# Attention with top-k and two gated MLPs on one core: keys stored once and queries split twice, a fold factor kept, weight stores on SP, another scheduler

## The chip, the cores and the metric

The kernel runs on one core of one Trainium2 chip. The metric is the device time in microseconds of one execution. A core has TensorE (PE, with its weight loads PEld), VectorE (DVE), ScalarE (ACT), GpSimd (POOL) and SyncE (SP), and 16 DMA engines that serve the transfers issued by SP and ScalarE.

## The reference

```python
# attention: q, k, v of (4, 8, 576, 64)
scores = scale * np.matmul(q, k.transpose(0, 1, 3, 2))
kth = np.partition(scores, -32, axis=-1)[..., -32:-31]
scores = np.where(scores >= kth, scores, -1000000000.0)
attn = np.exp(scores - max); attn = attn / (sum + 1e-09)
x = np.matmul(attn, v)            # heads side by side: (2304, 512)
# first MLP: w_in (512, 2048), w_out (2048, 512)
h = x @ w_in; x = (h * sigmoid(h)) @ w_out
# second MLP: w1, w2 (512, 1024), w3 (1024, 1024), w4 (1024, 512)
out = (((x @ w1) * (x @ w2)) @ w3) @ w4
```

For each query only the 32 largest scores of a row of 576 count. All is float32.

## The kernel before

The 2304 tokens are cut into six blocks of three row tiles of 128, that is 384 tokens each; a batch has 576 tokens, so blocks cross batches. For each block the eight heads' attention gives 24 (head, row tile) items, taken in 12 pairs; then comes the block's MLP work. The pairs' attention runs ahead: while block j goes through the MLPs, block j+1 goes through attention.

**Precision.** Most matmuls run in the format fp32r, with each operand split in a rounded part and a remainder; three products (rounded x rounded, rounded x remainder, remainder x rounded) give the result. For the scores the 64-wide heads leave half of the 128 partitions free: queries lie in tile `qs` with the rounded part in the lower 64 partitions and the remainder in the upper 64; keys lie in `kk` as two planes, rounded and remainder, each stored twice over the partitions. Two matmuls of 288 columns give half a row of scores. A batch's keys, where a later block needs them again, are written to DRAM (`kscr`) and read back into `kk` (`load_qk`, `cached_k`, `split_qk`, `go`).

**Top-k.** `plan_topk`: VectorE takes the 8 largest of a row four times (`mx`), erasing them in between (`mr`). ScalarE masks and exponentiates into `e`, VectorE adds and takes the reciprocal `rc` (`recip`), one for each pair. `norm` then makes ready what the transposes need.

**Attention output.** `plan_av`: `tr` transposes the probabilities on TensorE, `ev` evicts them, `mm` multiplies by v. Blocks 0 and 1 are "native": plain float32, with two heads' v in one tile `vn`. In block 0 (`DIAG`) a transpose is a matmul by the diagonal tile `dg` = identity x `rc`, which scales as it transposes; in block 1 `norm` scales `e` itself and a transpose by `ident` follows. The result becomes `xh` and `xl`, the MLP's input.

**Weights.** In block 0 the weights come raw from DRAM and are split by `conv_step(k)`: load (SP), two ScalarE passes, a GpSimd clamp, VectorE's joining of bits, ScalarE's rounding and GpSimd's subtraction into a piece `wt`. Each of the 48 finished pieces (512 KB) is stored to DRAM (`scr`) from ScalarE's queue and read back by all later blocks (`stream`). Loads of raw weights share a ring of four buffers (`RB`); pieces have two rings of three (`WT`, tags w0 and w1).

**Fold.** `fold_steps` computes w3 @ w4 once, in two halves of eight jobs, so the second MLP ends in one matmul less; its remainder is `w4l`. The factor w4 is converted in the first half, stored to DRAM (`scr4`, ScalarE's queue) and read back from SP into `w4r` for the second.

**Order.** All of this is recorded first as a list of operations with modelled costs (`Recorder`). `schedule` then looks for an order: `forward` is a list scheduler that gives start times from a rank, `backward` gives a new rank from these, and of 24 rounds the rank with the least sum of three jittered cases is kept. Instructions are emitted in the order of their start times, so each engine's queue, and SP's with all its loads, runs in that order. Line 457 of the profile is the line that emits them all; so the rows are told apart by tiles.

Of the kernel before, what the change touches and what calls it, by code (L numbers as in the profile page):

```python
# [29 lines left out]
KB = 3  # L30
# [8 lines left out]
ROUNDS = 24  # L39
CASES = 3  # L40
ENGINES = ("sync", "scalar", "vector", "gpsimd", "tensor")
WAKE = (17, 24, 24, 70, 44)
POOL, PE = 3, 4
NATIVE = lambda j: j < 2
# [165 lines left out]
class Recorder:  # L210
# [52 lines left out]
    def graph(self):  # L263
        ops = self.ops
        self.needs = [sorted(o.needs) for o in ops]
        self.heirs, self.after = [[] for _ in ops], [[] for _ in ops]
        index, self.key, self.turn, ahead = {}, [], [], {}
        self.users, self.takes = [], [[] for _ in ops]
        for n, o in enumerate(ops):
            for k in self.needs[n]:  # L270
                self.heirs[k].append(n)
            for k in sorted(o.weak):
                self.after[k].append(n)
            for t in o.takes:
# [8 lines left out]
        self.tiles = [[index[t] for t in o.tiles] for o in ops]  # L283
        self.engine = [ENGINES.index(o.engine) for o in ops]
        self.wake = [WAKE[e] for e in self.engine]

    def queues(self, rank, takes, turn, left, gap):
        given, spare = dict.fromkeys(self.caps, 0), {k: [0.] * c for k, c in self.caps.items()}
        got, parked, avail = [None] * len(self.key), {}, [0.] * len(self.ops)
        later, ready, free = [[] for _ in ENGINES], [[] for _ in ENGINES], [0.] * len(ENGINES)  # L290
        key, engine = self.key, self.engine

        def offer(n):
# [9 lines left out]
            for t in takes[n]:  # L303
                if got[t] is None:
                    got[t] = heapq.heappop(spare[key[t]])
                    given[key[t]] += 1
                if got[t] > 0.:
                    avail[n] = max(avail[n], got[t] + gap(n))
# [8 lines left out]
        def back(t, when):  # L317
            heapq.heappush(spare[key[t]], when)
            wake(key[t])
# [16 lines left out]

    def forward(self, rank, hold, done):
        ops, engine = self.ops, self.engine
        left = [len(o.needs) + len(o.weak) for o in ops]
        offer, back, pick, avail, free = self.queues(rank, self.takes, self.turn, left, lambda n: 0.)  # L340
        users, lastuse = [len(u) for u in self.users], [0.] * len(self.key)
        start, total = [0.] * len(ops), 0.
        wire = busy = held = 0.
        for _ in ops:
            t, e, ready = pick()
            n = heapq.heappop(ready)[1]
            late = 0.
            if ops[n].shares and busy > t + AVOID:
                aside = [n]
                while ready and ops[ready[0][1]].shares:  # L350
# [4 lines left out]
            if ops[n].shares:  # L355
                late = max(0., busy - t)
                held = t + late + hold[n]
            elif e == POOL:
                late = max(0., held - t)
                busy = t + late + hold[n]  # L360
            start[n] = t
            free[e] = t + late + hold[n]
            end = t + late + done[n]
            if ops[n].dma:
                wire = max(wire, t + 1400) + done[n]
                end = wire + 1050
            total = max(total, end)
# [58 lines left out]
    def jitter(self, dice, amount):  # L426
        hold, done = [], []
        for o in self.ops:
            f = 1. + amount * (2. * dice.random() - 1.)
            hold.append(o.hold if o.dma else o.hold * f + (0. if o.engine == "tensor" else 8.))  # L430
            done.append(o.done * (1. + 3. * amount * dice.random()) if o.dma else o.done * f + 8.)
        return hold, done

    def schedule(self):
        self.graph()
        dice = random.Random(7)
        cases = [self.jitter(dice, 0.04) for _ in range(CASES)]

        def cost(rank):
            return sum(self.forward(rank, *c)[1] for c in cases)  # L440

        rank = list(range(len(self.ops)))
        least = cost(rank)
        for _ in range(ROUNDS):
            times = self.jitter(dice, dice.choice((0., 0.02, 0.05)))
            r = rank
            for _ in range(2):
                r = self.backward(self.forward(r, *times)[0], *times)
                c = cost(r)
                if c < least:  # L450
                    least, rank = c, r
        start, _ = self.forward(rank, [o.hold for o in self.ops], [o.done for o in self.ops])
        return [self.ops[n] for n in sorted(range(len(start)), key=lambda n: (start[n], n))]

# [6 lines left out]
def attention_moe_moe2_kernel(  # L461
# [77 lines left out]

    def convert_bits(t, u, n=-1):  # L540
        w = raw_p.tile([128, 512], FP32, tag="w", bufs=WB, name="w")
        if MERGE(n):
# [19 lines left out]
    scr = [dram.tile([128, 2, 512], FP32, name=f"scr{i}") for i in range(NH)]  # L562
    scr4 = [dram.tile([128, DM], FP32, name=f"scr4_{i}") for i in range(NI)]
    piece = {}
# [10 lines left out]
    def conv_step(k):  # L575
# [23 lines left out]
    def fold_steps():  # L599
# [8 lines left out]
        st = {}  # L608
        cur = {}
        accs = []  # L610
# [3 lines left out]
        def mm(n):  # L614
            kind, half, j, _ = jobs[n]
            w = st.pop(n)
            if kind == "b":
                cur[j] = w
                nc.scalar.dma_start(out=scr4[j], in_=w)
                return  # L620
            if half == 0:
                b_ = cur.pop(j)
            else:
                b_ = cur.pop(("r", j))
            if j == 0:
# [17 lines left out]
        def step(k):  # L643
# [7 lines left out]
            if 0 <= a < len(jobs):  # L651
                st[a] = convert_bits(*st[a])
# [103 lines left out]
    def cached_v(j, h):  # L756
        t0, T = blocks[j]
        hd = heads[j, h]
        if NATIVE(j):
# [32 lines left out]
    def plan_scores(n, base):  # L792
# [9 lines left out]
        def go(tick, j, h, i, half, si, r0, r1):  # L802
# [498 lines left out]
```

## Time and profile before

| | us |
|---|---|
| median of 3 runs | 1127.8 (1127.1 to 1129.38) |
| profiled execution, its own time | 1130.65 |
| its span, first to last instruction | 1128.8 |
| TensorE busy | 1080.0 (96%) |
| VectorE busy | 898.1 (80%) |
| ScalarE busy | 851.6 (75%) |
| GpSimd busy | 745.1 (66%) |

In the rows, `out<-in` names the tiles that an instruction writes and reads, `xN` is a count, ACTq and SPq are the issues of transfers from ScalarE's and SP's queue. Issues are not in the engines' busy times. A matmul's end is modelled and neighbours overlap, so distances between starts say more than lengths.

### The profile page before, as it was taken

How to read it: one execution, taken by the hardware profiler on the slowest of the kernel's cores; microseconds unless marked ns; L12 is line 12 of the kernel's file. 1: busy time of each engine (PE TensorE's matmuls, PEld its weight loads, DVE VectorE, ACT ScalarE, POOL GpSimd, SP SyncE). 2: the span in 40 equal slices, each digit the busy share in tenths (PEclk: the TensorE clock that was granted, in tenths of full speed). 3: DMA queues.
4: the chain of work that ended last, by engine and by line, in shares of the span. 5: the costliest groups of instructions: out<-in, count | busy, mean ns of one | idle time of the engine just before them, and what ended most of it. 6: DMA issues, size and time to landing. Idle time of an engine off the chain costs nothing.

```text
span 1128.8 us, 19547 instructions
## 1 busy us (share of the span) xinstructions
PE 1080.0 (96%) x6096; PEld 983.9 (87%) x6096; DVE 898.1 (80%) x2062; ACT 851.6 (75%) x1911; POOL 745.1 (66%) x766
## 2 busy tenths in 40 slices
PE   4899997898899999999999999999999999999998
PEld 3555567787889999999999999999999999999997
DVE  7999999897979999998999988888899999401100
ACT  5899889888988878878878887888787788642221
POOL 4678557788886677867777766867766666542221
PEclk9899989999999999999999999999999999999999
DMA  8876479989898786767778667897857776358740
GB/s 278 255 251 217 136 251 313 304 299 353 278 325 318 240 239 211 268 195 233 249 265 284 232 198 249 295 311 275 280 169 256 244 235 197 131 159 253 252 167 28
DMA packets 127879, 273.53 MB, mean 242 GB/s; under 512 B 40480, under 2 KB 65056, under 8 KB 127776
## 3 DMA queue, kind: packets, MB, share of 16 engines
q1 hardware_dynamic: 119712, 245.02, 67.2%
q10 hardware_dynamic: 8064, 27.27, 6.1%
q8 instruction: 49, 0.80, 0.3%
q14 instruction: 54, 0.44, 0.1%
HBM read 216.14 MB, written 56.10 MB: 241 GB/s over the span
## 4 chain that ended last, share of the span: by engine, by line
PE 63%; DVE 17%; ACT 9%; POOL 5%; issue 4%; DMA 1%; ACTq 0%; SPq 0%; POOLq 0%; DVEq 0%
PE bank L457 63%; DVE top L457 7%; DVE wk L457 6%; ACT e L457 3%; DVE gf L457 2%; POOL wt L457 1%; ACT st L457 1%; POOL gl L457 1%; POOL t L457 1%; POOL e L457 1%; ACT t L457 1%; ACT wt L457 1%; ACT pf L457 0%; DMA raw<-in_w_dram 0%; ACT ph L457 0%
## 5 line engine op out<-in xcount | busy, mean ns | idle before, releaser
L457 DVE MAX8 top<-wk 128x8 f32<-128x576 f32 x432 | 319.5, 753 | 4.6
L457 POOL TENSOR_TENSOR gl<-gf,gh 128x384 fp32r<-128x384 f32 x144 | 147.6, 1025 | 165.7 <-ACT gh L457 159.9
L457 PE MATMUL bank<-xh,wt 128*128 128x384 f32 x768 | 221.4, 341 | 2.6 <-ACT st L457 2.6
L457 PE MATMUL bank<-gh,wt 128*128 128x384 f32 x768 | 221.9, 341 | 0.2 <-ACT gh L457 0.2
L457 PE MATMUL bank<-x2h,wt 128*128 128x384 f32 x768 | 217.3, 341 | 1.4 <-ACT wt L457 1.1
L457 DVE MATCH_REPLACE8 wk<-top,wk 128x576 f32<-128x576 f32 x288 | 213.4, 742 | 0.0
L457 PE MATMUL bank<-kk,qs 128*128 128x288 f32 x640 | 148.1, 321 | 21.8 <-ACT kk L457 12.0
L457 POOL TENSOR_TENSOR pl<-pf,ph 128x384 fp32r<-128x384 f32 x128 | 129.8, 1021 | 37.8 <-ACT ph L457 35.4
L457 ACT ACTIVATE st<-bank 128x288 f32<-128x288 f32 (+1 forms) x320 | 127.4, 410 | 34.3 <-PE bank L457 31.6
L457 PEld LDWEIGHTS bank<-kk,qs 128*128 128x128 f32 x640 | 114.6, 196 | 39.0 <-issue 11.0
L457 PEld LDWEIGHTS bank<-xh,wt 128*128 128x128 f32 x768 | 141.9, 189 | 3.5 <-ACT st L457 2.8
L457 PEld LDWEIGHTS bank<-x2h,wt 128*128 128x128 f32 x768 | 140.5, 188 | 4.1 <-ACT wt L457 1.3
L457 PEld LDWEIGHTS bank<-gh,wt 128*128 128x128 f32 x768 | 140.5, 189 | 1.6 <-ACT gh L457 0.6
L457 PE MATMUL bank<-gl,wt 128*128 128x384 f32 x384 | 131.5, 342 | 3.0 <-POOL gl L457 2.9
L457 DVE MAX8 top<-st 128x8 f32<-128x576 f32 x144 | 107.9, 751 | 31.5 <-ACT st L457 30.6
L457 PE MATMUL bank<-xl,wt 128*128 128x384 f32 x384 | 129.6, 338 | 1.1 <-POOL xl L457 1.1
L457 PE MATMUL bank<-x2l,wt 128*128 128x384 f32 x384 | 129.0, 337 | 0.3 <-POOL x2l L457 0.3
L457 ACT ACTIVATE e<-st,top 128x576 f32<-128x576 f32 x144 | 108.6, 777 | 21.4 <-DVE top L457 19.1
L457 POOL TENSOR_SCALAR e<-e,rc 128x640 f32<-128x640 f32 (+1 forms) x120 | 95.1, 801 | 40.7 <-DVE rc L457 17.5
L457 ACT CAST gh<-gf 128x384 fp32r<-128x384 f32 x144 | 74.2, 515 | 61.5 <-DVE gf L457 60.7
L457 ACT ACTIVATE e<-e,nb 128x576 f32<-128x576 f32 x144 | 111.7, 778 | 0.4 <-issue 0.3
L457 DVE SCALAR_TENSOR_TENSOR gf<-th,bank 128x384 f32<-128x384 f32 x96 | 52.4, 546 | 73.9 <-ACT th L457 72.1
(82 smaller groups left out, 2334.7 us busy)
## 6 DMA issues: line engine op xcount, KB each, us to landing
wt<-scr SPq DMA_DIRECT2D x240, 512.0 KB, 4.3
scr<-wt ACTq DMA_DIRECT2D x48, 512.0 KB, 5.4
k<-kk SPq DMA_DIRECT2D x32, 576.0 KB, 4.6
kk<-k SPq DMA_DIRECT2D x32, 576.0 KB, 5.3
raw<-in_w_dram SPq DMA_DIRECT2D x24, 512.0 KB, 5.6
kr<-in_kT_dram SPq DMA_DIRECT2D x32, 288.0 KB, 4.9
raw<-in_w3T_dram SPq DMA_DIRECT2D x16, 512.0 KB, 5.3
raw<-in_w_in_dram SPq DMA_DIRECT2D x16, 512.0 KB, 6.0
```

Source lines behind the costliest of these rows:

```text
L457: o.call(*[real_ap(x) for x in o.args], **{k: real_ap(x) for k, x in o.kw.items()})
```

## The change

- The scheduler: `forward` now takes the order in which buffers are handed out (`turns`) from the new rank, holds back a transfer while eight are under way, and doubles TensorE's times in stretches that follow little work. A new `replay` times a fixed order in four jittered cases, and the best order itself is kept (before, the best rank).
- Keys are one plane: rounded part in the lower partitions, remainder in the upper. Queries are two planes, rounded and remainder, each over all 128 partitions. A stored or reloaded `kk` has half the bytes.
- The fold's converted w4 stays in four `wt` tiles (`kept`); its stores and loads go.
- In `cached_v` one load fetches the last 64 rows of v for both heads.
- `DIAG` is false: block 0 scales `e` and transposes by identity, as block 1 does.
- The 48 stores of weight pieces are issued from SP.

```diff
-CASES = 3
+CASES = 4
+SEED = 8
+LANES = 8
...
-DIAG = lambda j: j == 0
+DIAG = lambda j: False
...
+STORE = lambda a: True
...
+    def turns(self, start):
+        turn, seen = [0] * len(self.key), {}
+        for t in sorted(range(len(turn)), key=lambda t: (start[self.taker[t]], self.taker[t], t)):
+            turn[t] = seen[self.key[t]] = seen.get(self.key[t], -1) + 1
+        return turn
...
+                if slow:
+                    h, d = 2. * h, d + h
+                filled += h
...
+            elif dma[n]:
+                late = max(0., lanes[lane] - t)
...
+                lanes[lane] = end = wire + 1050
+                lane = (lane + 1) % LANES
...
+    def replay(self, order, prior, hold, done, phase):
...
+        for n in order:
+            e = engine[n]
+            t, wake = free[e], wakes[n]
+            for k in self.needs[n]:
+                x = off[k] if e == PE and engine[k] == PE else end[k] + wake
+                if x > t:
+                    t = x
+            for x in self.takes[n]:
+                if prior[x] >= 0 and release[prior[x]] > t:
+                    t = release[prior[x]]
...
+        return total
 
     def schedule(self):
         self.graph()
-        dice = random.Random(7)
-        cases = [self.jitter(dice, 0.04) for _ in range(CASES)]
...
+        dice = random.Random(SEED)
+        cases = [self.jitter(dice, 0.03) for _ in range(CASES)]
+        plan, least, best = (list(range(len(self.ops))), self.turn), None, None
+
+        def trial(p, times):
+            nonlocal plan, least, best
+            start, _ = self.forward(p, *times)
+            order, prior = sorted(range(len(start)), key=lambda n: (start[n], n)), self.prior
+            c = sum(self.replay(order, prior, *x) for x in cases)
+            if least is None or c < least:
+                plan, least, best = p, c, order
+            return start
...
+            p = plan
             for _ in range(2):
...
+                rank = self.backward(trial(p, times), *times[:2])
+                p = rank, self.turns(rank)
+            trial(p, plain)
+        return [self.ops[n] for n in best]
...
-            nc.scalar.dma_start(out=scr[a], in_=piece[0, a].bitcast(FP32))
+            (nc.sync if STORE(a) else nc.scalar).dma_start(out=scr[a], in_=piece[0, a].bitcast(FP32))
...
-                cur[j] = w
-                nc.scalar.dma_start(out=scr4[j], in_=w)
                 return
...
+            b_ = kept[j // 2][:, j % 2]
...
-                if half == 1:
-                    b_ = wt_p.tile([128, 2, 512], FP32, tag=f"w{j % 2}", name="w4r")[:, 0]
-                    nc.sync.dma_start(out=b_, in_=scr4[j])
-                    cur["r", j] = b_
+                if kind == "b" and j % 2 == 0:
+                    kept.append(wt_p.tile([128, 2, 512], FP32, tag=f"w{j // 2 % 2}", name="w4f"))
+                st[a] = convert_bits(*st[a], w=kept[j // 2][:, j % 2] if kind == "b" else None)
...
-            kk = kv_p.tile([128, 2, S], FP32R, tag="k", bufs=KB, name="kk")
+            kk = kv_p.tile([128, S], FP32R, tag="k", bufs=KB, name="kk")
...
-        qs = kv_p.tile([128, T], FP32R, tag="qs", name="qs")
-        nc.scalar.copy(out=qs, in_=qr)
+        qs = kv_p.tile([128, 2, T], FP32R, tag="qs", name="qs")
+        nc.scalar.copy(out=qs[:, 0], in_=qr)
...
-        sub(out=qs[D:D2], in0=qr[D:D2], in1=qs[D:D2])
+        sub(out=qs[:, 1], in0=qr, in1=qs[:, 0])
...
-                nc.scalar.copy(out=kk[:, 0], in_=kr)
-                sub(out=kk[:, 1], in0=kr, in1=kk[:, 0])
+                nc.scalar.copy(out=kk, in_=kr)
+                sub(out=kk[D:D2], in0=kr[D:D2], in1=kk[D:D2])
                 if s + n < S:
-                    kscr[b, h] = dram.tile([128, 2, S], FP32, name=f"k{b}_{h}")
+                    kscr[b, h] = dram.tile([128, S], FP32, name=f"k{b}_{h}")
...
-                    nc.sync.dma_start(out=vt[0:REM, NFULL, x], in_=v[b, h + x, NFULL * 128:S])
+                nc.sync.dma_start(out=vt[0:REM, NFULL], in_=v[b, h:h + 2, NFULL * 128:S].rearrange("x p d -> p x d"))
...
-            q_ = hd["q"][:, i * 128:(i + 1) * 128]
-            nc.tensor.matmul(ps[:, 0:HS], lhsT=q_, rhs=kk[:, 0, cs], start=True, stop=False)
-            nc.tensor.matmul(ps[:, 0:HS], lhsT=q_, rhs=kk[:, 1, cs], start=False, stop=True)
+            for x in range(2):
+                nc.tensor.matmul(ps[:, 0:HS], lhsT=hd["q"][:, x, i * 128:(i + 1) * 128], rhs=kk[:, cs],
+                                 start=(x == 0), stop=(x == 1))
```

## Rows read from the trace of the kernel before

**Rows 1.** The page, part 1: busy us by engine, share of the span, instructions.

```profile
PE 1080.0 (96%) x6096; PEld 983.9 (87%) x6096; DVE 898.1 (80%) x2062; ACT 851.6 (75%) x1911; POOL 745.1 (66%) x766
```

**Rows 2.** Table by stage: stretch, length, busy us by engine, clock, DMA share, GB/s.

```profile
0.00:160.00 160.00, 137.38 (x538) 84.05 (x539) 148.90 (x348) 131.64 (x282) 99.34 (x109) 0.96 0.73 234
160.00:340.00 180.00, 158.94 (x892) 143.47 (x891) 156.50 (x334) 156.28 (x334) 147.85 (x143) 0.98 0.89 304
340.00:640.00 300.00, 299.95 (x1806) 290.91 (x1805) 280.95 (x660) 250.83 (x582) 223.78 (x231) 1.00 0.76 248
640.00:960.00 320.00, 318.58 (x1954) 307.95 (x1953) 283.82 (x664) 256.69 (x599) 219.82 (x229) 1.00 0.75 247
960.00:1128.00 168.00, 165.15 (x914) 157.47 (x912) 27.89 (x61) 56.18 (x118) 54.33 (x55) 1.00 0.52 166
```

**Rows 3.** Chain of waits from 0 to 160 us, shares by line.

```profile
by line: PE bank L457 70.5%; issue 4.2%; DMA raw<-in_w_dram 3.4%; POOL w L457 3.0%; DVE top L457 2.9%; ACT e L457 2.9%; DVE wk L457 2.7%; ACT st L457 2.7%; ACT t L457 1.5%; ACT pn L457 1.0%; ACT bank L457 0.8%; ACT wt L457 0.7%; SPq L457 0.
```

**Rows 4.** Chain of waits from 160 to 340 us, shares by line.

```profile
by line: PE bank L457 23.9%; issue 9.4%; POOL wt L457 8.6%; DVE top L457 5.4%; DVE wk L457 5.3%; POOL t L457 4.6%; ACT e L457 4.3%; POOL gl L457 3.9%; POOL e L457 3.6%; DMA k<-kk 2.8%; ACT wt L457 2.7%; ACT t L457 2.7%; ACT bank L457 2.3%; 
```

**Rows 5.** VectorE's timeline: start, length, the 12th and the 24th reciprocal.

```profile
156.28 0.14 DVE L457 RECIPROCAL rc<-rc 128x2 f32<-128x2 f32 x1
...
350.79 0.15 DVE L457 RECIPROCAL rc<-rc 128x2 f32<-128x2 f32 x1
```

**Rows 6.** Instructions of the tile xh: ns min/median/max, first and last start.

```profile
L457 PE MATMUL bank<-xh,wt x768: 331/334/656, 167.7 to 1069.1; 128*128 128x384 f32 x192
```

**Rows 7.** Groups by line, TensorE: count, busy us, mean ns, idle before.

```profile
L457 PE MATMUL bank<-ident,e 128*128 128x128 f32 x600 | 100.4, 274 | 7.9 <-ACT st L457 5.4 <-POOL e L457 1.5 <-ACT pn L457 0.7
...
L457 PE MATMUL bank<-dg,e 128*128 128x128 f32 (+1 forms) x240 | 35.8, 286 | 1.1 <-ACT st L457 1.0
```

**Rows 8.** TensorE's timeline at 68 us: start, length, what, count.

```profile
68.55 1.50 PE L457 MATMUL bank<-dg,e 128*128 128x128 f32 x12
69.80 0.51 PE L457 MATMUL bank<-kk,qs 128*128 128x288 f32 x2
```

**Rows 9.** Groups by line and shape, GpSimd and ScalarE, whole span.

```profile
L457 POOL TENSOR_TENSOR gl<-gf,gh 128x384 fp32r<-128x384 f32 x144 | 147.6, 1025 | 165.7 <-ACT gh L457 159.9 <-PE bank L457 4.3
...
L457 ACT ACTIVATE e<-st,top 128x576 f32<-128x576 f32 x144 | 108.6, 777 | 21.4 <-DVE top L457 19.1 <-POOL wt L457 1.3
...
L457 POOL TENSOR_TENSOR qs<-qr,qs 64x384 fp32r<-64x384 f32 x47 | 48.1, 1024 | 12.8 <-ACT qs L457 6.8 <-issue 3.1
...
L457 POOL TENSOR_SCALAR e<-e,rc 128x576 f32<-128x576 f32 x24 | 18.5, 778 | 4.6 <-ACT bank L457 2.1 <-DVE rc L457 1.4
...
L457 POOL TENSOR_SCALAR dg<-ident,rc 128x128 f32<-128x128 f32 x16 | 6.2, 394 | 7.7 <-DVE rc L457 7.0
...
L457 ACT ACTIVATE dg<-ident,rc 128x128 f32<-128x128 f32 x8 | 3.1, 407 | 0.0
```

**Rows 10.** Instructions of the tiles scr and w4l: ns min/median/max, first and last.

```profile
L457 ACTq DMA_DIRECT2D scr<-wt x48: 326/326/474, 144.4 to 360.1; - x48
...
L457 POOL TENSOR_TENSOR w4l<-wf,w4h x8: 1269/1277/1290, 93.4 to 141.6; 128x512 fp32r<-128x512 f32 x8
```

**Rows 11.** DMA issues between 160 and 340 us: count, KB each, us to landing.

```profile
scr<-wt ACTq DMA_DIRECT2D x40, 512.0 KB, 5.4
...
kk<-k SPq DMA_DIRECT2D x8, 576.0 KB, 6.4
k<-kk SPq DMA_DIRECT2D x6, 576.0 KB, 6.2
```

**Rows 12.** Waits between 160 and 340 us: total us, times, longest.

```profile
POOL t L457 <- ACT t L457: 8.3, 6, 4.5
DVE gf L457 <- ACT th L457: 8.2, 4, 3.7
...
DVE w L457 <- POOL t L457: 7.1, 8, 2.0
```

**Rows 13.** SP's timeline of issues at 215 us: start, length, what, count.

```profile
215.43 7.00 SPq L457 DMA_DIRECT2D vn<-in_v_dram  x6
```

More of the change, by code (lines that the diff above doesn't have):

```diff
@@ L43 @@
 POOL, PE = 3, 4
+WINDOW, FULL = 3413., 0.55
 NATIVE = lambda j: j < 2
-DIAG = lambda j: j == 0
+DIAG = lambda j: False
 EARLY = lambda j, h: j == 0 and h == 0
@@ L283, in graph @@
         self.tiles = [[index[t] for t in o.tiles] for o in ops]
+        self.taker = [n for n, o in enumerate(ops) for _ in o.takes]
+        self.shares = [o.shares for o in ops]
+        self.dma = [o.dma for o in ops]
         self.engine = [ENGINES.index(o.engine) for o in ops]
@@ L287, in queues @@
     def queues(self, rank, takes, turn, left, gap):
-        given, spare = dict.fromkeys(self.caps, 0), {k: [0.] * c for k, c in self.caps.items()}
+        given, spare = dict.fromkeys(self.caps, 0), {k: [(0., -1)] * c for k, c in self.caps.items()}
         got, parked, avail = [None] * len(self.key), {}, [0.] * len(self.ops)
+        prior = self.prior = [-1] * len(self.key)
         later, ready, free = [[] for _ in ENGINES], [[] for _ in ENGINES], [0.] * len(ENGINES)
@@ L304, in offer @@
                 if got[t] is None:
-                    got[t] = heapq.heappop(spare[key[t]])
+                    got[t], prior[t] = heapq.heappop(spare[key[t]])
                     given[key[t]] += 1
-                if got[t] > 0.:
+                if prior[t] >= 0:
                     avail[n] = max(avail[n], got[t] + gap(n))
@@ L317, in back @@
         def back(t, when):
-            heapq.heappush(spare[key[t]], when)
+            heapq.heappush(spare[key[t]], (when, t))
             wake(key[t])
@@ L335, in queues, with forward @@
         return offer, back, pick, avail, free
[L337 to L340, printed above, removed]
+    def turns(self, start):
[3 more added lines that the diff above has]
+        return turn
+    def forward(self, plan, hold, done, phase):
+        rank, turn = plan
+        engine, dma, shares = self.engine, self.dma, self.shares
+        left = [len(o.needs) + len(o.weak) for o in self.ops]
+        offer, back, pick, avail, free = self.queues(rank, self.takes, turn, left, lambda n: 0.)
         users, lastuse = [len(u) for u in self.users], [0.] * len(self.key)
-        start, total = [0.] * len(ops), 0.
+        start, total = [0.] * len(left), 0.
         wire = busy = held = 0.
-        for _ in ops:
+        window, filled, slow = 0, 0., True
+        lanes, lane = [0.] * LANES, 0
+        for _ in left:
             t, e, ready = pick()
@@ L347, in forward @@
             late = 0.
-            if ops[n].shares and busy > t + AVOID:
+            if shares[n] and busy > t + AVOID:
                 aside = [n]
-                while ready and ops[ready[0][1]].shares:
+                while ready and shares[ready[0][1]]:
                     aside.append(heapq.heappop(ready)[1])
@@ L354, in forward @@
                     heapq.heappush(ready, (rank[x], x))
-            if ops[n].shares:
-                late = max(0., busy - t)
-                held = t + late + hold[n]
+            h, d = hold[n], done[n]
+            if e == PE:
+                w = int((t + phase) // WINDOW)
+                while window < w:
+                    slow = filled < WINDOW * FULL
+                    filled = max(0., filled - WINDOW)
+                    window += 1
+                if slow:
+                    h, d = 2. * h, d + h
+                filled += h
             elif e == POOL:
                 late = max(0., held - t)
-                busy = t + late + hold[n]
-            start[n] = t
[L362 to L366, printed above, removed]
+                busy = t + late + h
+            elif shares[n]:
+                late = max(0., busy - t)
+                held = t + late + h
+            elif dma[n]:
+                late = max(0., lanes[lane] - t)
+            start[n] = t
+            free[e] = t + late + h
+            end = t + late + d
+            if dma[n]:
+                wire = max(wire, t + late + 1400) + d
+                lanes[lane] = end = wire + 1050
+                lane = (lane + 1) % LANES
             total = max(total, end)
@@ L431, in jitter @@
             done.append(o.done * (1. + 3. * amount * dice.random()) if o.dma else o.done * f + 8.)
-        return hold, done
+        return hold, done, dice.random() * WINDOW
+    def replay(self, order, prior, hold, done, phase):
+        engine, dma, shares, wakes = self.engine, self.dma, self.shares, self.wake
+        free, end, off = [0.] * len(ENGINES), [0.] * len(order), [0.] * len(order)
+        release = [0.] * len(prior)
+        wire = busy = held = total = 0.
+        window, filled, slow = 0, 0., True
+        lanes, lane = [0.] * LANES, 0
+        for n in order:
[8 more added lines that the diff above has]
+                    t = release[prior[x]]
+            h, d = hold[n], done[n]
+            if e == PE:
+                w = int((t + phase) // WINDOW)
+                while window < w:
+                    slow = filled < WINDOW * FULL
+                    filled = max(0., filled - WINDOW)
+                    window += 1
+                if slow:
+                    h, d = 2. * h, d + h
+                filled += h
+            elif e == POOL:
+                t = max(t, held)
+                busy = t + h
+            elif shares[n]:
+                t = max(t, busy)
+                held = t + h
+            elif dma[n]:
+                t = max(t, lanes[lane])
+            free[e] = off[n] = t + h
+            if dma[n]:
+                wire = max(wire, t + 1400) + d
+                lanes[lane] = end[n] = wire + 1050
+                lane = (lane + 1) % LANES
+            else:
+                end[n] = t + d
+            total = max(total, end[n])
+            for x in self.tiles[n]:
+                if end[n] + 45 > release[x]:
+                    release[x] = end[n] + 45
+        return total
@@ L434, in schedule @@
     def schedule(self):
         self.graph()
-        dice = random.Random(7)
-        cases = [self.jitter(dice, 0.04) for _ in range(CASES)]
[L439 to L443, printed above, removed]
+        dice = random.Random(SEED)
[9 more added lines that the diff above has]
+            return start
@@ L444, in schedule @@
+        plain = [o.hold for o in self.ops], [o.done for o in self.ops], 0.
+        trial(plan, plain)
         for _ in range(ROUNDS):
             times = self.jitter(dice, dice.choice((0., 0.02, 0.05)))
-            r = rank
+            p = plan
             for _ in range(2):
[L448 to L452, printed above, removed]
@@ L453, in schedule @@
-        return [self.ops[n] for n in sorted(range(len(start)), key=lambda n: (start[n], n))]
+                rank = self.backward(trial(p, times), *times[:2])
+                p = rank, self.turns(rank)
+            trial(p, plain)
+        return [self.ops[n] for n in best]
     def emit(self):
@@ L538, in convert_scale, with convert_bits @@
         return t, u
-    def convert_bits(t, u, n=-1):
-        w = raw_p.tile([128, 512], FP32, tag="w", bufs=WB, name="w")
+    def convert_bits(t, u, n=-1, w=None):
+        w = raw_p.tile([128, 512], FP32, tag="w", bufs=WB, name="w") if w is None else w
         if MERGE(n):
@@ L562, in attention_moe_moe2_kernel @@
     scr = [dram.tile([128, 2, 512], FP32, name=f"scr{i}") for i in range(NH)]
-    scr4 = [dram.tile([128, DM], FP32, name=f"scr4_{i}") for i in range(NI)]
     piece = {}
@@ L608, in fold_steps @@
         st = {}
-        cur = {}
+        kept = []
         accs = []
```

5 lines of the change are left out of this document (removed).

## The prediction

> **What bounds the kernel now.** I read the page first. TensorE is busy 96% of the span, VectorE 80% and ScalarE 75% [rows 1]. A busy time made of pipelined matmuls proves little, so the next view is the table by stage [rows 2]. It divides the run in two. From 340 us on TensorE idles 0.05 us of 300, then 1.4 of 320, then 2.9 of 168, at a clock of 1.00; nothing waits there that a better order could take away, and the change removes no matmul there. So the end moves only as far as work is brought forward before 340 us. There TensorE idles 22.6 us of the first 160 and 21.1 us of the next 180, and the clock is 0.96 and 0.98, which is another 6.4 + 3.6 us: 54 us in all are lost, and they are what the change can win from.
>
> The chain of waits says what holds each of these stages. In the first it runs over TensorE for 70.5% [rows 3], yet VectorE is busy 148.9 of 160 us [rows 2]. In the second TensorE has only 23.9% of the chain, and the rest is scattered over GpSimd's weight pieces, VectorE's top-k and ScalarE [rows 4]: no single engine binds, all are nearly full. VectorE's reciprocals, one for each pair of row tiles, give the pace: the 12th, the last of block 0, stands at 156.3 us and the 24th, the last of block 1, at 350.8 [rows 5]. The first MLP's first matmul follows at 167.7 us [rows 6].
>
> **The change part by part.** The sum is made against the profiled execution: 1130.65 us, its span of 1128.8 and 1.85 around it. The median of the runs is 1127.8, 2.85 lower.
>
> *Transposes by identity in block 0.* A matmul by the diagonal tile of float32 runs as two records: 240 for block 0's 120 transposes, where five other blocks have 600 records for 600 [rows 7]. In a dense stretch 12 records take 1.25 us from first start to the next item's start, 104 ns each [rows 8]. A native transpose has the same columns and one record, for which I take the same 104. So each transpose falls from 208 to 104 ns, and 120 of them give back 12.5 us of TensorE. What that is worth lies between 0 and 12.5. The chain speaks for the upper end, VectorE's fullness for the lower: block 0's MLP can't start before the 12th reciprocal, and VectorE idles 11.1 us in the stage, most of it before the first scores exist. I take 3 us, near the lower end, as VectorE's row is about the one thing the MLP must wait for.
>
> In exchange the whole probability tile is scaled instead of a 128-wide diagonal. On GpSimd 16 tiles go from 394 to 778 ns, 6.1 us in all; on ScalarE 8 tiles go from 407 to about the 777 of its nearest 576-wide row, 3.0 us [rows 9]. GpSimd is busy 99.3 of 160 us [rows 2] and hides its share; only the last tile's 0.4 us stands in the chain to the MLP. Bounds: 0.4 and, if ScalarE at 131.6 of 160 hides nothing, 0.4 + 3.0. I take a loss of 0.4.
>
> *Fold factor kept.* Eight stores of 256 KB leave ScalarE's queue (8 x 0.33 us = 2.6 us, by the like stores of [rows 10]) and eight loads leave SP's; 4.2 MB, about 18 us of transfer at the 234 GB/s of a stage where the DMA engines are busy 0.73 [rows 2]. That hides them, so I count 0, at best the 2.6 us of ScalarE. The kept tiles hold two of three slots in each piece ring until the fold ends, but in the trace no weight piece is worth having before: the last fold remainder is written at 141.6 us [rows 10], and block 0's MLP starts 26 us later. If the fold ended later, pieces would be late by as much.
>
> *Keys once, queries twice.* The score matmuls stay two for each half row, each with its own weight load as before, and a subtraction over 64 partitions costs what one over 128 does (1024 and 1025 ns [rows 9]); so no engine gains or loses. The stored keys halve. Between 160 and 340 us eight loads and six stores of 576 KB [rows 11] lose 288 KB each, 4.1 MB, which at 304 GB/s is 13.6 us out of the 160 us (0.89 of 180) for which the DMA engines are busy [rows 2].
>
> *Weight stores from SP.* Forty of the 48 fall in the same stage [rows 11]; at 326 ns each on ScalarE's queue [rows 10] that is 13.0 us. ScalarE's 156.3 busy us hold no issues, so it is really taken 169.3 of 180 us, 94%, and falls to 87%. SP gets the forty issues and their waits for GpSimd's subtraction; its loads stand behind them (rival 3).
>
> These two act on the two fullest resources of the second stage. Afterwards VectorE (156.5), ScalarE (156.3), GpSimd (147.9) and DMA (about 147) are the full ones, none above 87%. If the stage packs as tightly as ScalarE does now, it is 156.5 / 0.94 = 166.5 us long, a gain of 13.5. If VectorE's waits don't shrink, the gain is 0; but they are partly on ScalarE: 8.2 us for the tanh, and 7.1 for GpSimd's clamp, which itself waits 8.3 for ScalarE [rows 12]. I take 9.
>
> *One load for both heads' last rows of v.* It takes one of four issues from each fetch of a native block. Six issues of such loads took 7.0 us on SP in a stretch where the DMA engines were behind [rows 13]. I count it with the order of work.
>
> *The scheduler.* It now picks the order by replaying it with a queue of limited depth for transfers and with stretches of half-speed TensorE, in four jittered cases. Nothing in the trace prices it. Upper bound: half of the 43.7 us of idle, 22. Lower bound: the order after 340 us, with 4.4 us of idle in all, is as good as it can be, and can only be made worse; I allow 12. Nearest to a row is a stall such as that of the six loads, 7.0 us; the old plan didn't know of it. I take half of it with the v loads, 4.
>
> Sum: 3 - 0.4 + 0 + 9 + 4 = 15.6; 1130.65 - 15.6 = 1115.05, and 2.85 lower against the median: **1112 us**. Its own range follows if every term moves a third of the way to its bounds (together -15.4 and +50.2): 1101 to 1123. A change of 0.2%, 2.3 us, is about what can be told from none.
>
> **The rivals.**
> *1. All the relief counts.* If TensorE, and not VectorE, binds block 0, its 12.5 us come in full, the second stage gives 13.5 and the order some 10: 36 us, 1092. For it: the chain's 70.5%. Against it: VectorE's 148.9 of 160 us.
> *2. The relief is hidden.* VectorE's work before the 24th reciprocal is untouched by the change. If it alone sets the pace, only noise is left: 1128. Against it: its waits for ScalarE named above.
> *3. SP is held up (slower).* Every store must wait on SP for GpSimd's subtraction of its piece, and loads of raw weights, keys and queries stand behind it. SP has shown that it can stick: seven us for six issues [rows 13]. If half of a subtraction (1.3 us, as the fold's of the same size [rows 10]) is waited for at each of forty stores, raw loads come 26 us later in all, less the 9 gained: 1145; with a smaller wait, from 1131 on. It decides from about 0.25 us of wait for each store (forty times that is 10 us), if the four raw buffers hold no loads ahead. Against it: the issue order is planned with these waits in it.
> *4. TensorE's clock (slower).* In the first stage the clock is already 0.96. With half of the diagonal's records gone TensorE idles more there. If the clock fell to 1.2 GHz for half of the stage, at a mean of 0.75, about 160 x 0.21 = 34 us of its work would be lost against 22.6 us of idle and the 12.5 us saved; VectorE still paces, so I let a quarter of it show, 8 us: 1136. Against it: block 1's transposes are native and run in a stage at 0.98. The Trainium skill, page "TensorE: Matmul & The Clock Gate", section "Part 4: PE-mode transpose", speaks for it: a transpose-mode matmul does not count as busy for the clock gate in the way other matmuls do. By that rule block 0's transposes would help to lower the clock instead of holding it up, and the time would be that of this rival; the second stage's 0.98 doesn't bear it out so far, though weight matmuls stand between the transposes there.
>
> **How the numbers follow.** Forecast 0.55, rival 1 0.15, rival 2 0.12, rival 3 0.12, rival 4 0.06. Faster: 0.55 + 0.15 = 0.70; same 0.12; slower 0.12 + 0.06 = 0.18. A range of 1090 to 1134 leaves out a part of rival 1 (0.06) and most of rival 3 and a part of 4 (0.12); for the bounds of the scheduler's term I leave it there.
>
> **What would show it.** Right: TensorE's records for block 0's transposes fall to 120; DMA's bytes fall by some 23 MB (64 transfers lose 288 KB each, 16 of 256 KB go); no store is left on ScalarE's queue; the 24th reciprocal comes some 9 us earlier and the first MLP's first matmul about 3; behind that TensorE stays full. Wrong: the 24th reciprocal stays (rival 2); raw loads land later and GpSimd waits for ScalarE which waits for raw (rival 3); a clock well under 0.96 before 160 us (rival 4); or TensorE idling by more than 5 us after 340, which would be the scheduler's lower bound.

## The result and the profile after

The changed kernel takes 1116.15 us (median of four runs, 1114.36 to 1117.12) against 1128.59 before: ratio 0.9887, interval 0.9870 to 0.9905, 12.4 us faster. The forecast was 1112. The profiled execution is the fastest of the four, 1114.36 us with a span of 1112.6; that of before, 1130.65 us, is one of its slower ones. So the two traces lie 16.3 us apart, 3.9 more than the medians, and distances between them are too large by about that much.

The table by stage of the changed kernel (stretch, length, busy us of PE, PEld, DVE, ACT and POOL, clock, DMA share, GB/s):

```profile
0.00:160.00 160.00, 125.94 (x454) 72.65 (x454) 151.88 (x358) 140.74 (x296) 107.29 (x112) 0.96 0.63 193
160.00:340.00 180.00, 167.99 (x939) 153.15 (x939) 170.45 (x360) 163.66 (x349) 156.85 (x153) 0.97 0.88 296
340.00:640.00 300.00, 300.00 (x1799) 291.26 (x1798) 279.82 (x655) 247.33 (x577) 219.45 (x229) 1.00 0.73 229
640.00:960.00 320.00, 319.12 (x1964) 309.58 (x1964) 282.06 (x660) 256.88 (x597) 219.70 (x229) 1.00 0.69 223
960.00:1112.00 152.00, 148.90 (x826) 142.21 (x824) 15.93 (x31) 45.74 (x97) 45.98 (x46) 1.00 0.54 170
```

Against [rows 2]: from 340 to 960 us TensorE idles 0.9 us, so that part is as full as before. Before 340 the two stages moved apart. In the first TensorE works less (125.9 for 137.4 us) and VectorE, ScalarE and GpSimd more. In the second all engines are fuller: TensorE 168.0 for 158.9, VectorE 170.5 for 156.5, ScalarE 163.7 for 156.3, GpSimd 156.9 for 147.9. The DMA share of the first stage falls from 0.73 to 0.63, that of the second only from 0.89 to 0.88, because the same stretch now holds more of the work.

The chain of waits from 0 to 160 us, and from 160 to 340:

```profile
by line: DVE top L540 32.0%; DVE wk L540 27.0%; PE bank L540 11.5%; issue 6.0%; ACT e L540 4.9%; DVE w L540 4.2%; DMA raw<-in_w_dram 3.1%; ACT t L540 2.3%; ACT pn L540 1.6%; ACT st L540 1.6%; DVE w4f L540 1.2%; ACT bank L540 1.2%; DVE rc L5
...
by line: PE bank L540 27.5%; DVE wk L540 12.6%; DVE top L540 12.2%; issue 7.9%; DVE w L540 7.7%; ACT e L540 3.9%; DVE raw L540 3.4%; DVE gf L540 2.5%; ACT t L540 2.4%; ACT st L540 2.4%; POOL t L540 2.2%; POOL wt L540 2.1%; DMA raw<-in_w_out
```

In the first stage TensorE held 70.5% of the chain [rows 3] and now holds 11.5%; VectorE's top-k holds 59%. In the second VectorE's top-k rises from 10.7% [rows 4] to 24.8%. Shown next are VectorE's timeline (the 12th and the 24th reciprocal), the instructions of `xh` (ns min/median/max, first and last start) and the groups by line on TensorE:

```profile
150.40 0.15 DVE L540 RECIPROCAL rc<-rc 128x2 f32<-128x2 f32 x1
...
335.38 0.16 DVE L540 RECIPROCAL rc<-rc 128x2 f32<-128x2 f32 x1
```

```profile
L540 PE MATMUL bank<-xh,wt x768: 331/334/522, 162.7 to 1052.9; 128*128 128x384 f32 x192
```

```profile
L540 PE MATMUL bank<-ident,e 128*128 128x128 f32 (+1 forms) x720 | 119.3, 277 | 8.8 <-POOL e L540 8.3 <-ACT st L540 0.3 <-ACT e L540 0.2
```

The 12th reciprocal comes 5.9 us earlier than in [rows 5], the 24th 15.4, the first MLP's first matmul 5.0 [rows 6]. The span is 16.2 us shorter, so nearly all of the difference between the two traces is there by the 24th reciprocal. The 240 records by the diagonal are gone and the identity's rise from 600 [rows 7] to 720: 120 fewer.

DMA issues from 160 to 340 us (count, KB each, median us to landing), and SP's longest wait there (total us, times, longest):

```profile
scr<-wt SPq DMA_DIRECT2D x42, 512.0 KB, 5.5
raw<-in_w_dram SPq DMA_DIRECT2D x16, 512.0 KB, 6.1
...
kk<-k SPq DMA_DIRECT2D x9, 288.0 KB, 4.8
...
k<-kk SPq DMA_DIRECT2D x6, 288.0 KB, 4.0
```

```profile
SPq L540 <- POOL wt L540: 49.0, 31, 4.4
```

The 42 stores stand on SP's queue, key transfers have 288 KB and land in 4.8 and 4.0 us instead of 6.4 and 6.2 [rows 11]. SP waits 49.0 us for GpSimd's subtractions. The raw loads of w1 and w2 in this stretch (ns min/median/max, first and last start), before and after, are all the same issued some 7 us earlier:

```profile
L457 SPq DMA_DIRECT2D raw<-in_w_dram x15: 368/379/1520, 265.7 to 332.2; - x15
...
L540 SPq DMA_DIRECT2D raw<-in_w_dram x16: 368/384/882, 258.6 to 325.7; - x16
```

### The profile page after: what moved, and what is told of

Its sections match the earlier page's. It is cut to its first block, busy times and chain, and to the rows that moved or that the text cites. A ratio compares the mean times of both kernels' runs of the same rounds, so it can differ in the third digit from the quotient of the medians.

```text
span 1112.6 us, 19274 instructions
## 1 busy us (share of the span) xinstructions
PE 1061.9 (95%) x5976; PEld 968.9 (87%) x5976; DVE 900.1 (81%) x2062; ACT 854.3 (77%) x1911; POOL 749.3 (67%) x766
## 4 chain that ended last, share of the span: by engine, by line
PE 61%; DVE 24%; ACT 7%; issue 4%; POOL 3%; DMA 1%; SPq 0%; POOLq 0%; ACTq 0%; DVEq 0%
PE bank L540 61%; DVE top L540 11%; DVE wk L540 9%; ACT e L540 3%; DVE w L540 2%; DVE gf L540 1%; ACT st L540 1%; ACT t L540 1%; POOL e L540 1%; DVE raw L540 1%; DMA raw<-in_w_dram 0%; POOL t L540 0%; POOL gl L540 0%; ACT pf L540 0%; ACT wt L540 0%
## 5 line engine op out<-in xcount | busy, mean ns | idle before, releaser
L540 PEld LDWEIGHTS bank<-kk,qs 128*128 128x128 f32 x640 | 115.1, 197 | 42.6 <-POOL kk L540 13.4
L540 POOL TENSOR_SCALAR e<-e,rc 128x640 f32<-128x640 f32 (+1 forms) x136 | 108.1, 801 | 40.1 <-DVE rc L540 28.8
L540 PE MATMUL bank<-ident,e 128*128 128x128 f32 (+1 forms) x720 | 119.3, 277 | 8.8 <-POOL e L540 8.3
L540 PEld LDWEIGHTS bank<-ident,e 128*128 128x128 f32 (+1 forms) x720 | 91.5, 140 | 26.6 <-POOL e L540 10.3
```

What stands on the lines that cost most here:

```text
L540: o.call(*[real_ap(x) for x in o.args], **{k: real_ap(x) for k, x in o.kw.items()})
```

## The experiments

Ratios are to the kernel before, run on the same chip in the same session; 0.001 is 1.13 us. Each ratio is known to some 0.0017 either way, so a difference between two of them is known to some 0.0024, or 2.7 us (an estimate from the two intervals), and a smaller one can't be told from none.

### Which part brings the gain: the order or the edits

First the scheduler alone: the file before with the scheduler's parts of the diff, while keys, fold, v loads, stores and diagonal stay. Against the changed kernel:

```diff
-DIAG = lambda j: False
+DIAG = lambda j: j == 0
...
-            (nc.sync if STORE(a) else nc.scalar).dma_start(out=scr[a], in_=piece[0, a].bitcast(FP32))
+            nc.scalar.dma_start(out=scr[a], in_=piece[0, a].bitcast(FP32))
...
```

Then all the rest alone, with `forward` and `schedule` as they were. Against the changed kernel:

```diff
-CASES = 4
+CASES = 3
...
-        dice = random.Random(SEED)
-        cases = [self.jitter(dice, 0.03) for _ in range(CASES)]
+        dice = random.Random(7)
+        cases = [self.jitter(dice, 0.04) for _ in range(CASES)]
...
```

> The kernel before with the new scheduler alone; keys, fold, v loads, diagonal and ScalarE's stores as before. Relief theory (the prediction's own terms: order and v loads 4 us, all else from lighter DMA, ScalarE and TensorE): about 1125 us, ratio 0.997. Packing theory (the gain is that VectorE, the engine that sets the pace until the 24th reciprocal, is kept fuller by the new order; the other edits only relieve engines that didn't bind): 1116 to 1119 us, ratio about 0.990, with VectorE idling under 22 us of the first 340 where it idled 34.6 before.

> All edits but the scheduler: the old search finds an order for the new operations. Relief theory: about 1116 to 1119 us, ratio 0.990. Packing theory: within 3 us of before, ratio 0.998 to 1.002, VectorE still idling some 30 us of the first 340.

The scheduler alone: 1129.36 us, ratio 1.0001 (0.9989 to 1.0013), nothing. The edits alone: 1121.32 us, 0.9932 (0.9918 to 0.9946), 7.7 us faster. Together they give 0.9887. The packing theory fails on both counts. The relief theory, which had 4 and some 11 us, is nearer, but the scheduler's 4 us don't show either, and the edits alone are short of 11. The table by stage, of the scheduler alone and then of the edits alone:

```profile
0.00:160.00 160.00, 138.67 (x568) 84.38 (x569) 148.88 (x352) 137.63 (x294) 102.89 (x113) 0.99 0.75 242
160.00:340.00 180.00, 159.20 (x861) 145.49 (x860) 159.88 (x339) 153.76 (x326) 146.65 (x142) 0.93 0.89 304
```

```profile
0.00:160.00 160.00, 126.24 (x441) 71.05 (x442) 147.94 (x351) 136.42 (x289) 105.83 (x111) 0.95 0.61 184
160.00:340.00 180.00, 165.35 (x938) 150.02 (x936) 168.69 (x360) 164.41 (x353) 157.36 (x152) 0.99 0.88 302
```

With the new scheduler and the old operations the second stage is hardly fuller than in [rows 2] (VectorE 159.9 for 156.5). With the old scheduler and the new operations VectorE reaches 168.7 and TensorE 165.4 there. The room comes from the edits. One rival stays: with the scheduler alone the clock of the second stage is 0.93, for 0.98 before, so part of what its order could have gained may have been lost to the clock. That wasn't tried apart.

A second throw of the search's dice, with the edits and without:

```diff
-SEED = 8
+SEED = 9
```

> The changed kernel with the search's dice begun at 9 instead of 8: another order from the same scheduler, costs and edits. Theory that the scheduler itself is worth the 5 us by which the changed kernel beats the edits alone: within 2.5 us of the changed kernel, 1114 to 1119. Theory that these 5 us are the luck of one search (the scheduler alone brought nothing with the operations of before): 3 us or more slower, 1119 to 1124.

> The kernel before with the new scheduler alone, its dice begun at 9 instead of 8. With the edits, seed 9 beat seed 8 by 6 us. Theory that the scheduler brings nothing while the operations are those of before, whatever the dice: within 2.3 us of before, ratio 0.998 to 1.002. Theory that a search result scatters by some 5 us and seed 8 was unlucky here: 4 us or more faster than before, ratio 0.9965 or less.

With the edits: 1110.19 us, ratio 0.9834 (0.9818 to 0.9850), 6 us better than the changed kernel and the fastest kernel of this study, ahead of both. Neither expectation held. Without the edits: 1128.87 us, 0.9991 (0.9982 to 1.0001), again nothing. So with the operations of before two searches brought no gain, and with the edits two searches gave 5 and 11 us beyond the edits with the old search; between two orders of one scheduler lie 6 us. The old search was run only once with the edits, so how much of these 5 and 11 us is the scheduler and how much is the throw stays open.

### What each edit is worth with the order kept

A new search changes everything at once. So the next kernels keep the changed kernel's order: the positions that its search found stand in the file.

```diff
     def schedule(self):
         self.graph()
-        dice = random.Random(SEED)
...
+        best = kept_order()
         return [self.ops[n] for n in best]
```

Stores back on ScalarE's queue at the same places, and then keys in two planes:

```diff
             (nc.sync if STORE(a) else nc.scalar).dma_start(out=scr[a], in_=piece[0, a].bitcast(FP32))
+            nc.ops[-1].call = real.scalar.dma_start
```

```diff
-            kk = kv_p.tile([128, S], FP32R, tag="k", bufs=KB, name="kk")
+            kk = kv_p.tile([128, 2, S], FP32R, tag="k", bufs=KB, name="kk")
...
-        qs = kv_p.tile([128, 2, T], FP32R, tag="qs", name="qs")
+        qs = kv_p.tile([128, T], FP32R, tag="qs", name="qs")
...
```

> The changed kernel's order of all operations kept to the last one; only the 48 weight stores are issued from ScalarE's queue instead of SP's, at the same place in the order. ScalarE gets 48 x 0.33 = 15.6 us of issues back. Relief theory: 5 to 8 us slower than the changed kernel, 1121 to 1124, since ScalarE is busy 163.7 of 180 us in the second stage. Rival that the stores hold up SP: 2 us or more faster than the changed kernel. Packing theory: within 3 us of the changed kernel, 1114 to 1119.

> The changed kernel's order of all operations kept; keys lie in two planes and queries in one again, so each of the 64 key transfers moves 576 KB instead of 288. Engines do the same work. Relief theory: 4 to 6 us slower than the changed kernel, as 13.6 us of transfers come back in the second stage: 1120 to 1122. Packing theory: within 2.5 us of the changed kernel.

Stores: 1117.85 us, 0.9902 (0.9886 to 0.9918), about 1.7 us slower than the changed kernel. Planes: 1117.50 us, 0.9904 (0.9887 to 0.9921), about 1.9 us slower (some first matmuls read queries before their subtraction here, so a wait of the real kernel may be missing). Both intervals overlap that of the changed kernel; taken alone, neither cost is told from none, and both fall to the packing theory's figures, below the relief theory's. Then both at once:

> The changed kernel's order kept; both of the edits that the prediction gave 9 us together are undone: the 48 weight stores on ScalarE's queue and two planes of keys (576 KB for each key transfer). A first score matmul that the kept order puts before the queries' subtraction reads them unsplit, so scores are a little wrong; the work is the same. Undone one by one they cost 1.7 and 1.9 us. Prediction's term (DMA and ScalarE bind together, so either one holds the stage): 8 us or more slower than the changed kernel, ratio to before 0.995 or more. Theory that each was worth little: 3 to 4.5 us slower, ratio 0.991 to 0.993.

1123.14 us, 0.9948 (0.9931 to 0.9964): 6.9 us slower than the changed kernel, which is clear of the noise (the same first matmuls read too early here). The sum of the two is 3.6; the excess of 3.3 us hangs on four ratios, each known to some 0.0017, and is not clear of it. The second stage in the table by stage, with two planes alone and then with both, and the 24th reciprocal in VectorE's timeline, with the stores alone, the planes alone and both:

```profile
160.00:340.00 180.00, 166.19 (x925) 151.06 (x924) 165.76 (x353) 161.74 (x346) 154.16 (x150) 0.97 0.93 316
...
160.00:340.00 180.00, 164.70 (x907) 149.32 (x906) 162.51 (x345) 158.64 (x339) 150.73 (x147) 0.96 0.91 307
```

```profile
340.86 0.15 DVE L684 RECIPROCAL rc<-rc 128x2 f32<-128x2 f32 x1
...
338.59 0.16 DVE L684 RECIPROCAL rc<-rc 128x2 f32<-128x2 f32 x1
...
342.57 0.15 DVE L684 RECIPROCAL rc<-rc 128x2 f32<-128x2 f32 x1
```

With both, DMA is busy 0.91 of the stage, VectorE falls back from 170.5 to 162.5 us, and the reciprocal comes 7.2 us later than in the changed kernel. But in these traces, one execution each, the stores alone delay it by 5.5 us and the planes alone by 3.2, together more than 7.2, and the planes alone have DMA busy 0.93. So the two edits are worth something together, as the prediction had it; that each is worth little without the other is not shown.

The diagonal back in block 0, and the fold's factor stored after its first use and read back before its second (into the same tiles; the places of the sixteen transfers in the order are mine, not those of before):

```diff
-DIAG = lambda j: False
+DIAG = lambda j: j == 0
```

```diff
+            if half == 0:
+                nc.ops[-1].then = lambda: real.scalar.dma_start(out=scr4[j], in_=real_ap(b_))
...
+                if half == 1:
+                    nc.ops[-1].then = lambda b_=kept[j // 2][:, j % 2], j=j: real.sync.dma_start(out=real_ap(b_), in_=scr4[j])
```

> The changed kernel's order of all operations kept; block 0's transposes are matmuls by the diagonal again, 208 instead of 104 ns each on TensorE (+12.5 us), while the scaling falls from 778 to 394 ns on GpSimd and from 777 to 407 on ScalarE. Prediction's term (VectorE paces block 0, TensorE's 12.5 us are worth 3): 1 to 4 us slower than the changed kernel, 1117 to 1120. Rival 1 (TensorE binds block 0): 8 to 12 us slower, 1124 to 1128. Rival 4 (native transposes lower the clock): the clock before 160 us rises above 0.96 and the time falls.

> The changed kernel's order kept; the fold's eight factor tiles are stored to DRAM from ScalarE's queue after their first use and read back into the same tiles by SP before their second, 16 more transfers of 256 KB. Prediction's term (hidden, at best ScalarE's 2.6 us): 0 to 3 us slower than the changed kernel. If the transfers of the first stage bind after all: 5 us or more slower.

Diagonal: 1120.49 us, 0.9913 (0.9898 to 0.9928), 2.9 us slower, barely clear of the noise, inside the prediction's term and far from rival 1. Its first stage in the table by stage:

```profile
0.00:160.00 160.00, 135.71 (x556) 83.12 (x556) 149.37 (x349) 134.65 (x289) 99.73 (x110) 0.95 0.61 186
```

TensorE is busy 9.8 us more there and the clock is 0.95, not above the changed kernel's 0.96. Fold: 1120.43 us, 0.9919 (0.9901 to 0.9936), 3.6 us slower, just above what was expected, though with the noise not clearly. The fold's loads (instructions of the tile w4f: ns min/median/max, first and last start) and the 12th reciprocal in VectorE's timeline:

```profile
L883 SPq DMA_DIRECT2D w4f<-scr x8: 423/454/1507, 87.6 to 123.8; - x8
```

```profile
155.11 0.15 DVE L684 RECIPROCAL rc<-rc 128x2 f32<-128x2 f32 x1
```

The last factor is fetched at 123.8 us, and the 12th reciprocal comes at 155.1 instead of 150.4. The cost arises before the first MLP, then. I read it as the order's: a factor that comes late holds TensorE's queue, and what stands behind it is late too. TensorE's waits for these loads are 1.2 us, and they have 3.2% of the chain of waits from 0 to 160 us, 5.1 us. Loads, stores and their places weren't tried apart.

### Which engine sets the pace before 340 us

Two kernels take work away from one engine in blocks 0 and 1, the order kept: VectorE's third erasing pass (after `match_replace`), or ScalarE's masking pass. An operation with `times` 0 isn't issued, one with 2 is issued twice.

```diff
+                if r == 2 and n < 24:
+                    nc.ops[-1].times = 0
```

```diff
+                if n < 24:
+                    nc.ops[-1].times = 0
...
-                nc.scalar.activation(out=e, in_=e, func=ACTF.Exp, bias=st["nb"][:, i:i + 1],
+                nc.scalar.activation(out=e, in_=st["s"][:, i] if n < 24 else e, func=ACTF.Exp, bias=st["nb"][:, i:i + 1],
```

> The changed kernel's order kept; in the pairs of blocks 0 and 1 the third erasing pass is left out, so the fourth maximum finds the third's values again and the mask is wrong. VectorE has 48 x 0.83 = 39.6 us less work before the 24th reciprocal. Packing theory (VectorE paces until then): the 24th reciprocal comes 15 us or more earlier and the end 10 us or more. Theory that ScalarE, GpSimd and DMA pace the second stage together with it: the end comes less than 6 us earlier.

> The changed kernel's order kept; in the pairs of blocks 0 and 1 the masking pass is left out and the exponential reads the scores themselves, so every key counts. ScalarE has 48 x 0.78 = 37.4 us less work before the 24th reciprocal. VectorE's like relief of 39.6 us brought 2.7 us. Theory that ScalarE paces the first 340 us of the changed kernel: the 24th reciprocal at least 12 us earlier, the end 10 us or more. Theory that several engines run in lock step on the order (relief of any one is lost in the next wait): 1 to 5 us faster, the reciprocal within 5 us.

Lighter VectorE: 1114.40 us, 0.9863 (0.9847 to 0.9879), 2.7 us faster than the changed kernel. Lighter ScalarE: 1112.87 us, 0.9858 (0.9840 to 0.9877), 3.3 us faster. Both gains are at the edge of the noise. The first two rows of the table by stage and the 24th reciprocal, with the lighter VectorE and then with the lighter ScalarE:

```profile
0.00:160.00 160.00, 128.28 (x451) 74.08 (x452) 137.09 (x304) 139.33 (x295) 108.37 (x111) 0.94 0.62 191
160.00:340.00 180.00, 169.70 (x943) 154.01 (x941) 156.14 (x318) 164.15 (x350) 157.52 (x153) 0.97 0.88 298
```

```profile
335.56 0.16 DVE L685 RECIPROCAL rc<-rc 128x2 f32<-128x2 f32 x1
```

```profile
0.00:160.00 160.00, 129.02 (x456) 73.57 (x456) 153.46 (x361) 126.73 (x276) 107.75 (x112) 0.93 0.64 195
160.00:340.00 180.00, 169.30 (x952) 154.03 (x953) 171.23 (x363) 151.02 (x327) 159.49 (x154) 0.98 0.89 300
```

```profile
333.01 0.15 DVE L685 RECIPROCAL rc<-rc 128x2 f32<-128x2 f32 x1
```

VectorE is busy 14.8 and 14.3 us less in the two stages, together 29.1 and not the 39.6 that was expected from 48 records' lengths: the records overlap their neighbours. The reciprocal stays where it was (335.6 for 335.4 us). ScalarE is busy 26.7 us less, not 37.4, and the reciprocal comes 2.4 us earlier. So neither VectorE nor ScalarE alone paces these stages in this order. The chain of waits with the lighter VectorE, from 0 to 160 us and from 160 to 340:

```profile
by line: PE bank L685 35.2%; ACT e L685 13.3%; issue 7.2%; DVE top L685 5.8%; ACT st L685 4.4%; ACT t L685 4.0%; DMA raw<-in_w_dram 3.8%; DMA kr<-in_kT_dram 3.3%; ACT raw L685 3.0%; DVE wk L685 2.7%; ACT pn L685 2.3%; POOL t L685 1.7%; POOL
...
by line: PE bank L685 39.7%; ACT e L685 10.0%; issue 6.7%; ACT t L685 6.1%; ACT st L685 5.3%; ACT wt L685 4.2%; ACT bank L685 3.5%; POOL wt L685 2.3%; DMA qr<-in_qT_dram 1.9%; ACT th L685 1.9%; DMA raw<-in_w_in_dram 1.8%; POOL gl L685 1.7%;
```

VectorE's top-k falls from 59% of the first chain to 8.5%, TensorE rises to 35.2%, and the time hardly moves. TensorE, GpSimd and DMA were not made lighter, so whether one of them paces these stages stays open. Whether a search made for the lighter work would gain more wasn't tried.

The opposite, in blocks 3 and 4, where TensorE looks like the bound:

```diff
+                if r == 0 and 36 <= n < 60:
+                    nc.ops[-1].times = 2
```

> The changed kernel's order kept; in the pairs of blocks 3 and 4 the first maximum is taken twice, 48 x 0.75 = 36 us more for VectorE, in a part where TensorE idles under 1 us of 300. If VectorE has slack there (busy 280 of 300): up to 15 us slower; if VectorE's lead over TensorE is short: 15 to 25 us slower. No theory here has it at nothing, since VectorE idles only 38 us of the 320 from 640 us.

1147.22 us, 1.0152 (1.0138 to 1.0165): 29.9 us slower than the changed kernel for 36 us more of VectorE, beyond all that was expected. Its stages from 340 us:

```profile
340.00:640.00 300.00, 291.12 (x1725) 278.18 (x1724) 281.82 (x643) 236.35 (x554) 211.53 (x220) 1.00 0.70 220
640.00:960.00 320.00, 307.61 (x1852) 292.84 (x1851) 288.33 (x659) 241.26 (x563) 207.06 (x216) 0.99 0.67 217
```

TensorE, full before, now idles 8.9 and 12.4 us, and its work between 340 and 960 drops from 3763 to 3577 instructions. The added idle time, 20.4 us, is some two thirds of the cost; for the rest TensorE counts as busy, with longer records whose ends are modelled. A TensorE without idle time did not mean that VectorE had room. The order was made for the shorter work here too, and a new search wasn't tried.

## Why the prediction was right

The sum was 15.6 us, the measured gain 12.4. The signs came as named: DMA's bytes fall from 273.5 to 250.4 MB, 23 as predicted, and TensorE idles 0.9 us from 340 to 960. The 24th reciprocal comes 15.4 us earlier, for some 9, the first MLP 5.0, for about 3. The sizes of two terms and one reading were not right. That the total came so near is in part luck: one term was too small and one too large, and the parts don't add up, as shown at the end of this section.

- **Transposes, 3 - 0.4 us.** Undone with the order kept they cost 2.9, give or take 2.6. Rival 1, TensorE's 12.5 us in full, is refuted, though the chain's 70.5% spoke for it: a chain over TensorE in a stage where VectorE is busy 93% was no price. Nor was VectorE's 59% of the chain afterwards.
- **Fold, 0 us.** This term was mis-sized: "That hides them, so I count 0". The reload costs 3.6 us, give or take 2.8, with the transfers where I put them. A DMA share of 0.73 hides bytes; it says nothing of who waits for one of them.
- **Stores and keys, 9 us together.** 6.9 with the order kept, give or take 2.7, and 1.7 and 1.9 one by one, neither told from none. That the two are worth something was right; the size was perhaps somewhat high. That they must act together is not shown.
- **Scheduler and v loads, 4 us.** Beyond the edits alone the changed kernel gains 5.1; the scheduler without the edits gains nothing, for two seeds. The prediction added the term as if it stood by itself. Whatever it is worth, it was worth that only with the edits, and how much of the 5.1 is the throw of the search stays open. The v loads weren't measured alone.
- **VectorE paces until the 24th reciprocal.** This reading was too strong. Relief of VectorE by 29.1 us left the reciprocal where it was. Rival 2, by which VectorE alone sets the pace and nothing is gained, is refuted by the 12.4 us.
- **Rival 3, SP held up.** The price named was 0.25 us for each store as the point where it decides. SP waits 49.0 us, 1.2 for each of the 42 stores, and yet raw loads of w1 and w2 are issued earlier than before, not later, and land in 6.1 us, for 5.9; and stores on ScalarE's queue are no faster. The step that failed in the rival is that a wait on SP is a delay of the loads behind it: SP's queue waited before too, and the sum of its listed waits in the stage went from 133.5 to 122.3 us. The stores' waits took the place of others.
- **Rival 4, TensorE's clock.** 0.96 in the first stage before and after, 0.95 with the diagonal back. The rule of the Trainium skill, page "TensorE: Matmul & The Clock Gate", section "Part 4: PE-mode transpose", that a transpose-mode matmul doesn't count as busy for the clock gate in the same way, shows no effect on the clock here that could be told from the differences between orders. Among the orders run, the stage's clock lies between 0.89 and 0.99, and the fastest kernel (seed 9) has 0.89.

The edits undone with the order kept add up to 6.9 + 2.9 + 3.6 = 13.4 us, about the 12.8 us of the ratio. That is no proof that the parts are right one by one, since a kept order can punish an undoing: the same edits with an order of the old search gained 7.7.

## What to carry to other kernels

Where four engines are busy 85 to 95% of a stage, don't price the relief of one by its busy time: 29.1 us taken from VectorE gave 2.7, and 26.7 from ScalarE 3.3. Before crediting a new scheduler, run it with the old operations and with another seed; here it was worth nothing without the edits, and two orders of the same search differed by 6 us, half of the whole change's gain. Keep the order when you undo one part, and say that it can punish the undoing.

## What was not expected

In the changed kernel TensorE idles under 1 us of 620 from 340 to 960 us, while VectorE idles 20 of 300 and 38 of 320; and yet 36 us more on VectorE cost 29.9. In this order little of VectorE's idle time could be used, and only an added load showed it.
